# Retention and an ELU feed-forward layer on one core: the blank products at the beginning, and the place of one group of retention products

## The chip, the cores and the metric

The kernel runs on one core of a Trainium2 chip. Its time is the device time of one execution in microseconds (us). The kernel before has a median of 639.2 us over 13 runs, which lie between 636.57 and 641.93. Five engines work side by side: TensorE (PE in the profile; its weight loads are PEld) multiplies matrices, VectorE (DVE) and ScalarE (ACT) work on elements, GpSimd (POOL) does a little of the same, and SyncE (SP) issues the transfers.

## The reference

Two blocks follow one another. Both work in float32.

```python
# retention: q, k, v are (4, 8, 768, 64); one gamma per head
for t in range(S):
    state = gamma * state + einsum('bhd,bhe->bhde', k[:, :, t], v[:, :, t])
    y[:, :, t] = scale * einsum('bhd,bhde->bhe', q[:, :, t], state)
# feed-forward: x is y as (3072, 512)
h = x @ w_in                                        # 512 x 2048
g = np.where(h > 0, h, np.exp(np.minimum(h, 0)) - 1)
out = g @ w_out                                     # 2048 x 512
```

## The kernel before

**Work and stages.** The 3072 tokens are cut into six blocks of 512 (`tb` in the code), and each block into four chunks of 128. For a chunk, retention is computed in sub-chunks of 64 tokens, with products of 64x64: scores (`score_products`, L313), state increments (`state_products`, L344), the part of the output within a sub-chunk (`within`, L400), and the part that comes from the earlier state (`across`, L415). VectorE masks the scores (L324, L334), sums the states (L354, L356) and multiplies the output by powers of gamma into `xb` (L390, L439), which is the input of the feed-forward layer.

The two large products of a block use Strassen's scheme with seven products in place of eight. In the second product of blocks 1 to 5 it is applied twice (`second_twice`): an outer product `j` is made of seven inner ones (`inner`, L955), each of four 128x128 matmuls with weights that were combined before, sent to DRAM and brought back through a ring of eleven buffers (`fetch_small`). VectorE makes the inner inputs (`ts`, L832) and adds the results (L967); ScalarE copies out of PSUM (L963, L988). Between outer products VectorE also combines four inputs (`next_input`, L775).

**What sets the order.** The schedule is manual: each engine executes its instructions in the order in which the Python code emits them, and semaphores between engines follow from the tiles. Generators interleave the stages by hand. The outer products run in the order `ORDER2 = [1, 2, 6, 7, 5, 3, 4]`. `second_twice` yields after each outer product; at such a yield the main loop may place retention work of the next block, a "visit", by `retention_step`. Of an outer product, five inner products come before its yield, and the last two come after the first two of the next. Between two successive yields lie seven inner products.

`retention_step(tb, step)` has five steps: 0 makes the scores, 1 the states. Steps 2, 3 and 4 advance the output: step 2 makes the products L400 and the first half of L415 for the first pair of chunks, with a tiny copy (`seen`, L384) by VectorE that reads both banks; step 3 does the same for the second pair; step 4 makes the second half of L415 for both pairs and the final multiplications (L390). In the loop over blocks 2 to 5, steps 2, 3, 4 for the next block are at the yields numbered 1, 3, 5 of the second product; block 5 has no next block, so this happens three times. Block 1 has a loop of its own with other places, and block 0 another second product.

**The beginning.** No weights are ready at the start: they come as float64 bits in pieces (`load_piece`), which ScalarE and VectorE turn into float32 (L168, L170, L172, L194, L195, L198). TensorE begins with `unread`: products of a tile of zeros (`blank`) whose result nothing reads. Two of 512 columns stand before the scores of chunk 0, one of 256 before its states, and two more of 512 stand further on. Then come the products of chunks 0 and 1, and the plain first product of block 0 (`plain_first`, L503 and L527).

Of the kernel before, what the change touches and what calls it, by code (L numbers as in the profile page):

```python
# [18 lines left out]
def kernel(  # L19
# [32 lines left out]
    nc = tc.nc  # L52
    PSUM = bass.MemoryType.PSUM
    P = nc.NUM_PARTITIONS

    B, H, S, D, DM, DFF = dims
    NTOK = B * S
    C = P
    TB = 512
# [39 lines left out]
    def load(m):  # L99

        if m >= NCHUNK:
            return
        for which in range(2):
            load_one(m, which)
# [106 lines left out]
    blank = hpool.tile([P, TB], FP32, name="blank", tag="h")  # L211
# [69 lines left out]
    def scale_v(m):  # L281
        if m >= NCHUNK:
            return
        i = chunks[m][1]
        qk, kv = raw[m]
        eng = nc.vector if m < 2 else nc.gpsimd
        eng.tensor_tensor(  # L287
            out=kv[:, 1], in0=kv[:, 1], in1=vf[:, i].unsqueeze(2).to_broadcast([C, H, D]), op=ALU.mult
        )
# [28 lines left out]
    def scores(tb, pp):  # L318

        sc = [ps_r.tile([P, 2, HP, D], FP32, name="sc", tag="r") for _ in range(2)]  # L320
        for x in range(2):
            score_products(sc, tb, pp, x)
        for a in range(2):
            nc.vector.tensor_tensor(  # L324
                out=raw[tb * CPB + 2 * pp + a][0][:, 1].rearrange("p h c -> p (h c)").rearrange("p (n t) -> p n t", t=D),
                in0=sc[a].rearrange("p x h t -> p (x h) t"),
                in1=cmask.unsqueeze(1).to_broadcast([P, 2 * HP, D]), op=ALU.mult,
            )
# [29 lines left out]
    def states(tb, pp):  # L358

        kvs = [ps_r.tile([P, 2, HP, D], FP32, name="kv", tag="r") for _ in range(2)]  # L360
        for x in range(2):
            state_products(kvs, tb, pp, x, range(2))
        for x in range(2):
            for sub in range(2):
                state_sum(kvs, tb, pp, x, sub)
# [80 lines left out]
    def outputs_step(tb, step):  # L446

        if step == 0:
            held["y"] = [outputs(tb, pp) for pp in range(2)]
        if step < 2:  # L450
            next(held["y"][step])
            next(held["y"][step])
        else:
            for g in held["y"]:
                next(g, None)
# [3 lines left out]
    def combine_x_parts(tb=None):  # L459
        sub = lambda o, x, y: nc.vector.tensor_tensor(out=o, in0=x, in1=y, op=ALU.subtract)  # L460
        b11, b12, b21, b22 = (x_of(tb)[:, 2 * r : 2 * r + 2, half[t]] for r in range(2) for t in range(2))
        t1, t2, t3, t4_ = xt1 if tb == 1 else xt
        sub(t1, b12, b11)
        yield
        sub(t2, b22, t1)
        yield
        sub(t3, b22, b12)
        yield
        sub(t4_, b21, t2)
# [4 lines left out]
    def flush():  # L474
        while later:
            later.pop(0)()
# [214 lines left out]
    def bank(x):  # L691
        return ps_f.tile([P, 2, TH], FP32, name="p" + x, tag=x, bufs=2 if x == "a" else 1)

    def kept(ps):
        m = mpool.tile([P, 2, TH], FP32, name="m", tag="m")
        nc.scalar.copy(m, ps)  # L696
        return m
# [210 lines left out]
    def first_rest(n, j, ps):  # L908

        w, x = {  # L910
            1: (w_a[n][:, :, 0], xb[:, 0:2, half[0]]), 6: (w_s[n][:, 0], xt[1]), 5: (w_b[n][:, :, 0], xt[0]),
            4: (w_b[n][:, :, 1], xt[3]), 7: (w_s[n][:, 1], xt[2]),
        }[j]
        for fi in range(2):
            for j2 in range(2):
                nc.tensor.matmul(  # L916
                    ps[:, fi, :], lhsT=w[:, fi, j2, :], rhs=x[:, j2, :],
                    start=(j in (1, 7) and fi == 0 and j2 == 0), stop=(j2 == 1), skip_group_check=True,
                )

    def first_end(n, name, ps, x=None):

        g = gq[name][:, 2 * n : 2 * n + 2, :]
        nc.vector.tensor_tensor(out=g, in0=ps, in1=g if x is None else x, op=ALU.add)  # L924
        g = g.rearrange("p a b -> p (a b)")

        def combine():
            mine = lambda x: gq[x][:, 2 * n : 2 * n + 2, :].rearrange("p a b -> p (a b)")
            sub = lambda o, x, y: nc.vector.tensor_tensor(out=o, in0=x, in1=y, op=ALU.subtract)
            sub(mine("T3"), mine("C22"), mine("C12"))  # L930
            sub(mine("T1"), mine("C12"), mine("C11"))

        return lambda: elu(g, g, 3, combine if name == "C22" else None)
# [164 lines left out]

    warm = bank("a").rearrange("p a b -> p (a b)")

    def unread(count, n):
        for _ in range(count):
            nc.tensor.matmul(warm[:, 0:n], lhsT=blank[:, 0:P], rhs=blank[:, 0:n], start=True, stop=True, skip_group_check=True)

    unread(2, TB)
    sc = [ps_r.tile([P, 2, HP, D], FP32, name="sc", tag="r") for _ in range(2)]
    score_products(sc, 0, 0, 0)
    scale_v(0)
# [14 lines left out]
    mask_pair(sc, 1)  # L1123
    scale_v(1)
    unread(1, TB)
    inner = plain_first()
    next(inner)
# [125 lines left out]
    def retention_step(tb, step):  # L1253
        if tb >= NTB:
            return
        if step == 0:
            scores(tb, 0)
            scores(tb, 1)
        elif step == 1:
            states(tb, 0)  # L1260
            states(tb, 1)
        elif step < 5:
            outputs_step(tb, step - 2)
# [51 lines left out]
    for tb in range(2, NTB):  # L1315
        more = tb + 1 < NTB
        qa, qd, u2, end = {}, {}, {}, None

        def rest(n, j):
            if j == 1:  # L1320
                qa[n] = ps_r.tile([P, 2, TH], FP32, name="qa", tag="r") if n == 0 else bank("a")
            if j == 7:
                qd[n] = ps_r.tile([P, 2, TH], FP32, name="qd", tag="r") if n == 3 else bank("bd"[n % 2])
            first_rest(n, j, qa[n] if j in (1, 6, 5) else qd[n])

        def bring(n):
            if more:
                load((tb + 1) * CPB + n)
                scale_v((tb + 1) * CPB + n)

        def pop(count=1):
            for _ in range(count):
                if later:
                    later.pop(0)()

        bring(0)
        rest(0, 1)
        for _ in tail:
            pass
        tail, parts = iter(()), combine_x_parts()  # L1340
        for at, j in enumerate(TWICE):
            cur = first_twice(tb, j)

            next(cur)
            next(tail, None)
            next(parts, None)
            next(cur)
            for _ in tail:
                pass
            next(parts, None)  # L1350
            if at == 1:

                first_end(0, "C11", qa[0])()
                bring(1)
            next(cur)
            tail = cur
        next(tail)
        bring(2)

        sec = second_twice(tb, combine_x_twice if more else lambda: None)  # L1360
        for n in range(NQ):

            rest(n, 6)
            u2[n] = kept(qa[n])
            if n == 0:
                for _ in tail:
                    pass
            if end:
                end()
            pop()  # L1370
            rest(n, 7)
            m7 = kept(qd[n])
            pop(2)
            if n == 2 and more:
                retention_step(tb + 1, 1)
            if n == 3:
                next(sec)
            rest(n, 5)
            end = first_end(n, "C12", qa[n])
            other = first_end(n, "C22", qa[n], m7)  # L1380
            if n < 3:
                end()
                other()
                rest(n + 1, 1)
                first_end(n + 1, "C11", qa[n + 1])()
                rest(n, 4)
                end = first_end(n, "C21", qd[n], u2[n])
                pop()
                if n == 0:
                    bring(3)  # L1390
                elif n == 1 and more:
                    retention_step(tb + 1, 0)
        for _ in range(2):
            next(sec)
        end()
        other()
        rest(3, 4)
        end = first_end(3, "C21", qd[3], u2[3])
        next(sec)
        end()  # L1400
        flush()
        for step, s in enumerate(sec):

            if step in (1, 3, 5):
                retention_step(tb + 1, 2 + step // 2)
            if s == ORDER2[-1]:
                break
        tail = sec
# [51 lines left out]
```

## Time and profile before

| What | Value |
|---|---|
| Median of 13 runs | 639.2 us |
| The profiled execution | 637.46 us |
| Its span, first to last instruction | 635.7 us |
| TensorE products | 626.2 us busy (99%), 6626 records |
| TensorE weight loads | 560.0 us busy (88%) |
| VectorE | 483.0 us busy (76%) |
| ScalarE | 252.8 us busy (40%) |
| GpSimd | 40.3 us busy (6%) |
| Transfers | 136.84 MB, mean 215 GB/s |

The profile shows one execution. A timeline line gives the start, the duration, the engine, the line of the kernel, the operation, the tiles (result <- operands) and shapes, the number of merged records, and in brackets the idle time before it with what ended it. A float32 product makes two records of matmul and two of weight load. Durations of matmuls include their latency, so records overlap: the pace is read from the starts. "issue" is time in which an engine waited for nothing that the profile shows.

### The profile page before, as it was taken

The numbers are of one execution on the slowest core, as the hardware profiler recorded it, in microseconds if no ns is written. First come the engines' busy times: TensorE is split into PE (matmuls) and PEld (weight loads), VectorE is DVE, ScalarE is ACT, GpSimd is POOL, SyncE is SP. The second block draws the span as 40 slices with busy tenths as digits, with TensorE's granted clock in tenths as the row PEclk, the third lists the DMA queues.
The fourth block names the chain that finished last, engine by engine and source line by source line (L and its number), as shares of the span: only waits on it lengthen the run. The fifth ranks groups of instructions, "written<-read, shape, count | busy, mean of one in ns | idle before, by whom it ended". The sixth has DMA issues, their size and how long they took to land.

```text
span 635.7 us, 16093 instructions
## 1 busy us (share of the span) xinstructions
PE 626.2 (99%) x6626; PEld 560.0 (88%) x6626; DVE 483.0 (76%) x870; ACT 252.8 (40%) x472; POOL 40.3 (6%) x42
## 2 busy tenths in 40 slices
PE   8899999999999999999999999999999999999998
PEld 5765568888889999889999989999988999988997
DVE  5769979978989675589676598767489859558975
ACT  6689735114551113554112546111465211356311
POOL 1102000000820000200000100000110000000000
DMA  8789876688486888505889802889820688700794
GB/s 294 305 334 347 279 208 194 203 236 270 139 296 195 277 246 291 218 3 152 276 257 311 282 3 67 254 278 301 293 89 12 205 272 273 233 21 1 222 312 163
DMA packets 79209, 136.84 MB, mean 215 GB/s; under 512 B 6688, under 2 KB 32160, under 8 KB 76960
## 3 DMA queue, kind: packets, MB, share of 16 engines
q1 hardware_dynamic: 79136, 135.82, 65.4%
q8 instruction: 52, 0.85, 0.5%
q14 instruction: 21, 0.17, 0.1%
HBM read 114.56 MB, written 21.23 MB: 214 GB/s over the span
## 4 chain that ended last, share of the span: by engine, by line
PE 95%; DMA 2%; DVE 1%; issue 1%; ACT 1%; SPq 0%; POOL 0%; DVEq 0%
PE pa L955 20%; PE pa L916 10%; PE pd L955 10%; PE pb L955 5%; PE pa L870 5%; PE pb L916 4%; PE pa L527 3%; PE pa L746 3%; PE qa L916 3%; PE x L617 3%; PE pd L870 2%; PE qd L916 2%; PE pa L617 2%; PE pd L916 2%; PE y L400 2%; PE sc L313 2%
## 5 line engine op out<-in xcount | busy, mean ns | idle before, releaser
L963 ACT COPY ms<-pa 128x128 f32<-128x128 f32 x104 | 27.6, 265 | 146.8 <-PE pa L955 145.2
L955 PE MATMUL pa<-ts,wq 128*128 128x128 f32 x560 | 74.1, 275 | 0.3 <-ACT ms L963 0.3
L955 PE MATMUL pd<-ts,wq 128*128 128x128 f32 x552 | 73.2, 275 | 0.0
L955 PEld LDWEIGHTS pa<-ts,wq 128*128 128x128 f32 x560 | 68.5, 192 | 0.8 <-ACT ms L963 0.5
L955 PEld LDWEIGHTS pd<-ts,wq 128*128 128x128 f32 x552 | 67.1, 192 | 0.3 <-DVE res L967 0.2
L955 PE MATMUL pa<-gC,wq 128*128 128x128 f32 x480 | 65.0, 278 | 0.9 <-issue 0.9
L484 ACT ACTIVATE r<-r 128x512 f32<-128x512 f32 x96 | 60.5, 631 | 3.1
L955 PEld LDWEIGHTS pa<-gC,wq 128*128 128x128 f32 x480 | 59.1, 192 | 2.5 <-issue 1.1
L483 ACT ACTIVATE r<-gC 128x512 f32<-128x512 f32 x64 | 39.9, 624 | 32.9 <-DVE gC L924 32.9
L967 DVE TENSOR_TENSOR res<-pd,ms 128x128 f32<-128x128 f32 x68 | 19.5, 287 | 36.8 <-PE pd L955 35.6
L287 POOL TENSOR_TENSOR kvn<-kvn,vf 128x512 f32<-128x512 f32 x22 | 26.1, 1192 | 312.8 <-DMA kvn<-in_qkv_dram 202.4
L487 DVE SCALAR_TENSOR_TENSOR gC<-r,gC 128x512 f32<-128x512 f32 x64 | 44.9, 734 | 0.7 <-ACT r L484 0.7
L832 DVE TENSOR_TENSOR ts<-gC,ts 128x512 f32<-128x512 f32 x60 | 41.3, 688 | 1.0
L832 DVE TENSOR_TENSOR ts<-gC 128x512 f32<-128x512 f32 x60 | 41.0, 684 | 0.0
L955 PE MATMUL pb<-gC,wq 128*128 128x128 f32 x240 | 32.8, 277 | 0.1
L988 ACT COPY res<-pa 128x128 f32<-128x128 f32 x34 | 9.0, 265 | 56.2 <-PE pa L955 54.7
L955 PEld LDWEIGHTS pb<-gC,wq 128*128 128x128 f32 x240 | 29.5, 192 | 0.8 <-DVE gC L487 0.8
L696 ACT COPY m<-pa 128x512 f32<-128x512 f32 x24 | 13.9, 579 | 29.8 <-PE pa L916 13.5
L924 DVE TENSOR_TENSOR gC<-qa,gC 128x512 f32<-128x512 f32 x8 | 5.5, 692 | 25.0 <-PE qa L916 18.3
L916 PE MATMUL pa<-xt,w_b 128*128 128x256 f32 x96 | 23.0, 382 | 0.0
L916 PE MATMUL pa<-xt,w_s 128*128 128x256 f32 x96 | 23.0, 382 | 0.0
L916 PE MATMUL pa<-xb,w_a 128*128 128x256 f32 x96 | 22.7, 379 | 0.0
(253 smaller groups left out, 1251.9 us busy)
## 6 DMA issues: line engine op xcount, KB each, us to landing
wq<-scratch_dram SPq DMA_DIRECT2D x277, 256.0 KB, 4.4
wraw<-in_w_dram SPq DMA_DIRECT2D x15, 1024.0 KB, 7.0
qk<-in_qkv_dram SPq DMA_DIRECT2D x24, 512.0 KB, 6.8
kvn<-in_qkv_dram SPq DMA_DIRECT2D x24, 512.0 KB, 7.4
out_dram<-res SPq DMA_DIRECT2D x14, 256.0 KB, 4.4
scratch_dram<-gT SPq DMA_DIRECT2D x12, 256.0 KB, 4.3
scratch_dram<-m SPq DMA_DIRECT2D x12, 192.0 KB, 6.0
scratch_dram<-so SPq DMA_DIRECT2D x4, 512.0 KB, 4.5
```

Source lines behind the costliest of these rows:

```text
L287: eng.tensor_tensor(out=kv[:, 1], in0=kv[:, 1], in1=vf[:, i].unsqueeze(2).to_broadcast([C, H, D]), op=ALU.mult)
L483: nc.scalar.activation(e, h, AF.Relu, scale=-1.0)
L484: nc.scalar.activation(e, e, AF.Exp, scale=-1.0)
L487: nc.vector.scalar_tensor_tensor(g, e, -1.0, h, ALU.add, ALU.max)
L527: nc.tensor.matmul(hp, lhsT=w[n][:, fi, j // 2, j % 2, :], rhs=xb[:, j, :], start=(j == 0), stop=(j == 3))
L617: nc.tensor.matmul(X[j][:, d, :], lhsT=w[j][:, d * P : d * P + P], rhs=x[j], start=(n == 0 and d == 0), stop=at_end, skip_group_check=True,)
L832: sub = lambda o, x, y: nc.vector.tensor_tensor(out=o, in0=x, in1=y, op=ALU.subtract)
L870: nc.tensor.matmul(ps[:, f, :], lhsT=lhs[f], rhs=xs[j][k], start=(begin and f == 0), stop=True, skip_group_check=True,)
L916: nc.tensor.matmul(ps[:, fi, :], lhsT=w[:, fi, j2, :], rhs=x[:, j2, :], start=(j in (1, 7) and fi == 0 and j2 == 0), stop=(j2 == 1), skip_ ...
L955: nc.tensor.matmul(ps, lhsT=w[:, f, :], rhs=ts[j][k][:, f, :], start=(begin and f == 0), stop=(f == 3), skip_group_check=True,)
L963: nc.scalar.copy(m, ps)
L967: nc.vector.tensor_tensor(out=o, in0=x, in1=y, op=ALU.add)
```

## The change

There are two edits. In the first, `unread` takes the size of the quadratic blank weights as an argument `k`. Of the two 512-column blank products at the very beginning the first stays. In place of the second stand 28 products of 64 rows, 64 columns of weights and 64 moving columns. All 28 read the same corner of `blank` and write the same corner of the same PSUM bank. In the second edit, retention step 3 of the next block moves in the second product of blocks 2, 3 and 4 from the yield numbered 3 to the yield numbered 4; steps 2 and 4 stay at yields 1 and 5.

```diff
-    def unread(count, n):
+    def unread(count, n, k=P):
         for _ in range(count):
-            nc.tensor.matmul(warm[:, 0:n], lhsT=blank[:, 0:P], rhs=blank[:, 0:n], start=True, stop=True, skip_group_check=True)
-
-    unread(2, TB)
+            nc.tensor.matmul(
+                warm[0:k, 0:n], lhsT=blank[0:k, 0:k], rhs=blank[0:k, 0:n], start=True, stop=True, skip_group_check=True
+            )
+
+    unread(1, TB)
+    unread(28, D, D)
     sc = [ps_r.tile([P, 2, HP, D], FP32, name="sc", tag="r") for _ in range(2)]
     score_products(sc, 0, 0, 0)
     scale_v(0)
...
         for step, s in enumerate(sec):
 
-            if step in (1, 3, 5):
-                retention_step(tb + 1, 2 + step // 2)
+            if step in (1, 4, 5):
+                retention_step(tb + 1, {1: 2, 4: 3, 5: 4}[step])
             if s == ORDER2[-1]:
                 break
         tail = sec
```

In the order of TensorE's instructions, the 48 products of step 3 (32 of L400 and 16 of L415; 32 and 12 for block 4, whose first sub-chunk of a sequence has no earlier state) now come 28 matmuls of L955 later. On VectorE, the two copies L384 come behind the four combinations L832 of the next outer product. The orders of ScalarE, GpSimd and SyncE stay as they are.

## The prediction

> **What bounds the kernel now.** I read the page's busy row first, then the start and the second matrix product in the timeline, then the chain that ended last, and then the waits.
>
> ```profile
> PE 626.2 (99%) x6626; PEld 560.0 (88%) x6626; DVE 483.0 (76%) x870; ACT 252.8 (40%) x472; POOL 40.3 (6%) x42
> ...
> q8 instruction: 52, 0.85, 0.5%
> ```
>
> TensorE is busy for 626.2 of 635.7 us, so a change gains or loses only where TensorE idles, or by giving it more to do. Second line: 52 packets of instructions came in, 0.85 MB, about 16 KB each. TensorE runs 13,506 instructions (6,626 products, as many weight loads, 254 others)[...].
>
> The start, in the timeline (start, duration, engine, line, tiles, shape):
>
> ```profile
> 1.45 3.78 PE L1103 MATMUL pa<-blank 128*128 128x512 f32 x4 [1.45 <-DVE blank L212]
> 5.16 1.13 PE L313 MATMUL sc<-qk 64*64 64x64 f32 x32
> 6.22 0.87 PE L1103 MATMUL pa<-blank 128*128 128x256 f32 x2
> 7.03 0.69 PE L344 MATMUL kv<-kvn 64*64 64x64 f32 x32
> ...
> 8.30 0.45 PE L415 MATMUL pd<-qk,kvn 64*64 64x64 f32 x8
> ...
> 11.49 1.12 PE L503 MATMUL pa<-xb,w_a 128*128 128x128 f32 x8
> ```
>
> The two large blank products are four records (float32 takes two passes). Passes two to four start 0.853 us apart; the last leaves the array at 5.02, and the scores (L313) follow at 5.16. At 7.03 the state products (L344) wait for VectorE's scaling of v (L287, 6.22 to 6.91), and that for its load. All before about 6.5 us runs at half speed: 32 small products take 1.13 us at 5.16 but 0.69 at 7.03, though the granted clock reads 1.00 in every row.
>
> The only long idle times of TensorE, in the chain in order of time:
>
> ```profile
> 25.40 1.07 PE y L400 x58
> 26.47 1.72 issue
> 28.20 0.28 PE y L400 x3
> ```
>
> ```profile
> 503.84 0.98 PE pa L955 x7
> 504.81 0.94 issue
> ```
>
> "issue" means that no semaphore explains the wait. By start stamps the losses are 1.9 us (26.25 to 28.19) and 1.1 us (504.54 to 505.75). In the packet records of the instruction queue, a packet begins at 25.67 and lasts 1.07, another at 503.32 and lasts 0.92; both idle times end 1.5 us after their packet. Counting TensorE's instructions, these two stops and a 0.2 us one ending at 14.22 fall on counts equal modulo 256. They are waits for code[...].
>
> The second matrix product, around the visit that moves:
>
> ```profile
> 315.65 1.16 PE L400 MATMUL y<-qk,kvn 64*64 64x64 f32 x64
> 316.63 0.65 PE L415 MATMUL y<-qk,kvn 64*64 64x64 f32 x32
> 317.21 1.16 PE L955 MATMUL pa<-gC,wq 128*128 128x128 f32 x8
> ...
> 320.89 1.06 PE L955 MATMUL pa<-ts,wq 128*128 128x128 f32 x8
> ...
> 329.91 1.15 PE L415 MATMUL y<-qk,kvn 64*64 64x64 f32 x56
> ```
>
> ```profile
> 316.02 0.68 DVE L832 TENSOR_TENSOR ts<-gC,ts 128x512 f32<-128x512 f32 x1
> ...
> 317.31 0.24 DVE L384 COPY seen<-y 128x8 f32<-128x8 f32 x2 [0.41 <-PE y L415]
> ...
> 325.82 0.69 DVE L832 TENSOR_TENSOR ts<-gC,ts 128x512 f32<-128x512 f32 x1
> ```
>
> TensorE takes a product every 0.89 us without a hole, on both sides of the visit.
>
> **The change, part by part.**
>
> *Blank products.* Removed: two passes of 0.853, 1.71 us. Added: 28 float32 products, 56 passes, all on one 64x64 quarter. Such a stream is not in the trace. Floor: the four-quarter stream of L313, (1.13-0.31)/31 = 0.026 us a pass (0.31 is one record's latency), 1.5 us, no delay. Ceiling: weight load and product in turn, twice 0.107, 12 us at half speed. L313 gives each quarter 8 of its 32 passes, with starts within a quarter 0.107 us apart; at full speed (L344) 0.058. The two-quarter stream at 8.30 takes longer per pass than the four-quarter one, so the quarter is the limit, and loads are hidden in all of them. I take 0.107. Starting at 3.46 (free at 3.32 plus the 0.14 seen at 5.02 to 5.16), with the clock rising at 6.5 as now, 28 passes run slow and 28 at 0.058: end about 8.1, scores 8.2, **3.0 us late**.
>
> What covers it: the scores run at full speed and the state products waited until 7.03 for v anyway. Scores end 8.7, the blank 256-column product (0.43 warm) 9.1, so L344 is at 9.1, 2.1 late, and VectorE's first "seen" copy at 10.7 instead of 8.80. Behind that copy VectorE is nearly continuous to 11.33 (L439 twice, L356, L195, L198), and L503 at 11.49 needs the last of these. So **+1.9 us** reaches the first matrix product. The 0.44 wait for the second q, k load at 9.9 does not cover it, as VectorE decides.
>
> *Code blocks.* 27 more products, four instructions each: 108. Every later block boundary falls 108 instructions earlier in the work. [...] The rows show 3.0 us lost, so I count it:
> - At 26 us: the boundary moves 54 passes forward, to the start of the y burst, needed at 25.4+1.9 = 27.3. [...] I take 1.0, so 0.9 is given back.
> - [...] It is now needed after 3.4: +0.4.
> - At 504.5: the boundary before moves from about 499 to 493, with 9.7 us to the next instead of 5.2. Stall gone: -1.1.
> - Near 200: a boundary moves from after the state burst to before it[...]. Between 0 and +1.4; I take +0.4[...].
> - All other gaps stay above 5 us[...]: +0.1.
>
> *The visit, three times.* 48 products (1.55 us) go behind the seven products of the next visited step (6.25 us). Same instructions, same two changes of array shape, no DMA of its own; the weight loads that SP issues behind those products go out 1.55 us sooner, against landings of 4.4 us with 11 buffers: hidden. Those seven products now start at 315.65. The first that reads VectorE's new sums (pa<-ts) moves from 320.9 to 319.3; its last sum (L832) ends at 316.7: 2.6 us to spare. The copies of L384 go behind the L832 ending at 326.5, less up to 1.5; they are read from 329.9: over 3 us to spare. The L967 queued behind them feeds a bank reused two products later. The final multiplications (L390) stay in place. **0**; without that cover a late L384 would cost its lateness, at most about 1 us per block. Bounds -0.3 to +0.5 in all.
>
> *Sum* in the profiled execution's time: +1.9 -0.9 +0.4 -1.1 +0.4 +0.1 = **+0.8**, so 635.7 becomes 636.5 of span and 637.46 becomes 638.3. The median of the runs lies 1.7 above that execution; the difference carries over: **639.2 + 0.8 = 640.0 us**. A measurement tells about 0.2% (1.3 us) from no change, so this counts as no change.
>
> **The rivals.**
> 1. *The clock stays low* (slower). If products on one quarter do not count as enough activity, all 56 passes take 0.107 and end at 9.45, and scores, states and y run at half speed behind them: "seen" at 13.9, +5.1. Then loads are ahead and the 26 us stall goes: 5.1-1.9-1.1+0.5 = +2.6, **641.8**. For it: the low clock itself. Against: [...] no row here shows a quarter alone. It decides once the rise slips past 9.4; each microsecond before that costs 0.46.
> 2. *Code waits come back* (slower). The y burst stalls 2.0, the next block 0.8, the burst at 200 1.4: 1.9+0.1+0.8-1.1+1.4 = +3.1, **642.3**. [...]
> 3. *Code waits vanish* (faster). The new boundaries meet no burst: 1.9-1.9-0.2-1.1 = -1.3[...]: **637.6**. If the small products stream at the floor instead, there is no delay and the same side is reached: the edit is then a mere move of boundaries.
>
> **How the numbers follow.** Forecast (640.0) 0.36, its own range 638.6 to 640.9; rival 1 0.20, rival 2 0.18, rival 3 0.26. Faster is rival 3, slower is 1 and 2: 0.26, 0.36, 0.38. One in ten lies below 636.8, within rival 3, and one in ten above 642.7, within 2.
>
> **What would show it.** Right: L313 near 8.2 and L503 (128x128) near 13.4; an issue wait of about 1 us moved to the front of the y burst near 27; none at 504; visits without holes. Wrong: L313 near 5.2 (floor), or 64x64 records still long after 9 us (rival 1); issue waits over 1 us near 200 or 330 (rival 2); any VectorE wait ahead of L415 or pa<-ts near 320. Failing first would be the single-quarter pace or the arrival at 27, which I inferred rather than saw.

## The result and the profile after

The changed kernel takes **643.7 us** (median of 11 runs, 642.24 to 644.53) against 639.82 for the kernel before (48 runs, 636.25 to 642.28). The ratio is **1.0066, with a 95% interval of 1.0048 to 1.0085**: slower by 4 us, outside the predicted range. The profiled execution took 644.97 us with a span of 643.1, which is 7.4 us more span than before.

The 7.4 and the 4 differ because the mean granted clock of TensorE differs between executions. The profiled execution after had one stretch of 3.413 us (207.91 to 211.32 in the clock's records) at half the clock, and a mean of 0.997; half of that stretch, 1.7 us, is the estimate of its cost. The kernel before had a mean of 0.997 or lower in 64 of the 114 runs measured beside the experiments, the changed one in 2 of 12. The profiled execution of before had 1.000. Runs of before with that clock lie near 637.1 (median of 14, measured together with e5), those of the changed kernel near 643.8 (10 of 12). So at an equal clock the change costs about 6.7 us, and the profiled execution after, about 5.8 without its stretch.

The busy row and the instruction queue of the page after:

```profile
PE 633.8 (99%) x6680; PEld 567.5 (88%) x6680; DVE 483.3 (75%) x870; ACT 252.7 (39%) x472; POOL 39.7 (6%) x42
...
q8 instruction: 53, 0.87, 0.5%
```

TensorE is busy 7.6 us longer, so the loss lies in busy time rather than in waits, which nearly balance. The 56 small passes at full speed would be 56 x 0.058 = 3.2 us, less the 1.7 of the large ones, or 1.5; e5 below shows 3.0 us of the rest to be the low clock at the start, and 1.6 more are the half clock near 208 us. There is one more packet of instructions (53 for 52).

The start, in the timeline of after:

```profile
1.45 8.13 PE L1103 MATMUL pa<-blank 128*128 128x512 f32 x57 [1.45 <-DVE blank L212]
9.28 0.38 PE L313 MATMUL sc<-qk 64*64 64x64 f32 x3
9.38 0.31 PE L1103 MATMUL pa<-blank 64*64 64x64 f32 x1
9.44 1.10 PE L313 MATMUL sc<-qk 64*64 64x64 f32 x29
10.47 1.22 PE L1103 MATMUL pa<-blank 128*128 128x256 f32 x2
11.62 1.13 PE L344 MATMUL kv<-kvn 64*64 64x64 f32 x32
...
13.38 0.41 PE L415 MATMUL pd<-qk,kvn 64*64 64x64 f32 x8
...
16.51 1.13 PE L503 MATMUL pa<-xb,w_a 128*128 128x128 f32 x8 [0.49 <-DVE w_a L198]
```

VectorE's first `seen` copy, before and after:

```profile
8.80 0.16 DVE L432 COPY seen<-pd 128x4 f32<-128x4 f32 x1 [0.55 <-PE pd L415]
```

```profile
13.83 0.16 DVE L432 COPY seen<-pd 128x4 f32<-128x4 f32 x1 [0.55 <-PE pd L415]
```

The state products (L344) took 0.69 before and take 1.13 now, and the blank product of 256 columns 1.22 where it took 0.87: half speed. The clock's records say full speed from 13.35 us. L415 at 13.38 is the first group that runs about as before (0.41, before 0.45). VectorE's `seen` copy starts at 13.83 instead of 8.80, and the first matrix product at 16.51 instead of 11.49: 5.0 us late.

The chain around the y burst, and the visit in the second product of block 2:

```profile
28.71 1.92 PE pd L503 x8
30.64 1.09 PE y L400 x64
```

```profile
329.54 1.06 PE L955 MATMUL pa<-ts,wq 128*128 128x128 f32 x8
330.53 1.16 PE L400 MATMUL y<-qk,kvn 64*64 64x64 f32 x64
...
332.09 1.16 PE L955 MATMUL pa<-gC,wq 128*128 128x128 f32 x8
```

The wait of 1.7 us inside the y burst is gone altogether. The moved visit has no hole on either side. What is new comes near 206 us:

```profile
203.90 2.07 PE L344 MATMUL kv<-kvn 64*64 64x64 f32 x110
207.53 0.27 PE L344 MATMUL kv<-kvn 64*64 64x64 f32 x2 [1.55 <-issue]
207.73 1.94 PE L955 MATMUL pa<-gC,wq 128*128 128x128 f32 x8
...
211.16 1.13 PE L955 MATMUL pa<-gC,wq 128*128 128x128 f32 x8
```

A burst of 56 small products, 112 passes, stops after 110 passes for a wait that no semaphore explains, and behind it TensorE is granted half its clock for 3.413 us (207.91 to 211.32 in the clock's records): eight passes of L955 take 1.94, and 1.13 once the clock is back.

With start times of the same products subtracted (after minus before; places are times of the kernel before), the difference grows like this: scores +4.12, first matrix product +5.02, at 19.4 us +5.29, behind the y burst +3.2, at 190 us +5.2 (0.58 at 54, 0.33 at 67, 0.39 at 79, 0.60 at 181, all at small waits or their edges), behind the wait at 206 and the half clock +8.6, behind 504.5 us +7.4, and so to the end.

### The profile page after: what moved, and what is told of

It reads as the page before. It is cut to its first block, busy times and chain, and to the rows that moved or that the text cites. A ratio compares the mean times of both kernels' runs of the same rounds, so it can differ in the third digit from the quotient of the medians.

```text
span 643.1 us, 16201 instructions
## 1 busy us (share of the span) xinstructions
PE 633.8 (99%) x6680; PEld 567.5 (88%) x6680; DVE 483.3 (75%) x870; ACT 252.7 (39%) x472; POOL 39.7 (6%) x42
## 4 chain that ended last, share of the span: by engine, by line
PE 90%; DVE 3%; ACT 2%; issue 2%; POOL 1%; DMA 1%; POOLq 0%; SPq 0%; DVEq 0%
PE pa L955 20%; PE pa L916 10%; PE pd L955 9%; PE pb L955 5%; PE pa L870 5%; PE pb L916 4%; PE qa L916 3%; PE x L617 3%; PE pa L527 2%; PE pd L870 2%; PE qd L916 2%; PE pd L916 2%; PE pa L617 2%; PE kv L344 2%; PE y L400 2%; PE sc L313 2%
## 5 line engine op out<-in xcount | busy, mean ns | idle before, releaser
L955 PE MATMUL pa<-ts,wq 128*128 128x128 f32 x560 | 74.1, 275 | 0.3 <-ACT ms L963 0.3
L955 PE MATMUL pd<-ts,wq 128*128 128x128 f32 x552 | 73.1, 275 | 0.0
L955 PEld LDWEIGHTS pa<-ts,wq 128*128 128x128 f32 x560 | 68.5, 192 | 0.8 <-ACT ms L963 0.5
L955 PEld LDWEIGHTS pd<-ts,wq 128*128 128x128 f32 x552 | 67.1, 192 | 0.3 <-DVE res L967 0.2
L955 PE MATMUL pa<-gC,wq 128*128 128x128 f32 x480 | 65.6, 280 | 0.4 <-DMA wq<-scratch_dram 0.4
L955 PEld LDWEIGHTS pa<-gC,wq 128*128 128x128 f32 x480 | 59.8, 194 | 2.0 <-issue 0.7
L287 POOL TENSOR_TENSOR kvn<-kvn,vf 128x512 f32<-128x512 f32 x22 | 25.5, 1164 | 321.6 <-DMA kvn<-in_qkv_dram 295.7
L832 DVE TENSOR_TENSOR ts<-gC,ts 128x512 f32<-128x512 f32 x60 | 41.3, 688 | 1.0
L832 DVE TENSOR_TENSOR ts<-gC 128x512 f32<-128x512 f32 x60 | 41.0, 684 | 0.0
L955 PE MATMUL pb<-gC,wq 128*128 128x128 f32 x240 | 33.7, 282 | 0.1
L955 PEld LDWEIGHTS pb<-gC,wq 128*128 128x128 f32 x240 | 30.4, 197 | 0.8 <-DVE gC L487 0.8
L696 ACT COPY m<-pa 128x512 f32<-128x512 f32 x24 | 13.9, 579 | 30.0 <-PE pa L916 13.7
```

Source lines behind the costliest of these rows:

```text
L287: eng.tensor_tensor(out=kv[:, 1], in0=kv[:, 1], in1=vf[:, i].unsqueeze(2).to_broadcast([C, H, D]), op=ALU.mult)
L955: nc.tensor.matmul(ps, lhsT=w[:, f, :], rhs=ts[j][k][:, f, :], start=(begin and f == 0), stop=(f == 3), skip_group_check=True,)
```

## The experiments

The question that the profile leaves is how the start (+5.0) divides into the time of the small products and the low clock, what keeps the clock low, and whether the waits further on come from the number of instructions. "Start" below is the start of the scores, "seen" VectorE's first copy; differences are taken against the profiled execution of before.

### e2 and e1: one edit alone

```diff
-            if step in (1, 3, 5):
-                retention_step(tb + 1, 2 + step // 2)
+            if step in (1, 4, 5):
+                retention_step(tb + 1, {1: 2, 4: 3, 5: 4}[step])
```

> The visit alone, the start as before. If the clock at the start is the cause: within 0.3% of the kernel before (-1 to +1 us), no holes in TensorE around the visits. If the moved visit is the cause: +2 us or more, with VectorE waits ahead of the products L955 or L415 near 320, 420 and 520 us.

The visit alone (e2): 638.36 against 639.13, ratio 1.0003 (0.9982 to 1.0024), end of the profile -0.06 us. **The visit costs nothing.** The end alone would not show it, for two waits cancel there: a wait of 1.36 us at 13.8, in the products of block 0, where the kernel before had 0.22 (+1.1), and the wait at 504.5 us, which was absent (-1.2). But the difference stays at +1.15 from 215 to 500 us, over two of the three moved visits, and at -0.05 over the third. The wait at 504.5 was also absent in e8, e10 and e11, where the code is not shifted by 108 instructions: it is not a steady part of the kernel before, and its loss is no gain of the shift.

```diff
-    unread(2, TB)
+    unread(1, TB)
+    unread(28, D, D)      # unread with k, as in the change
```

> The blank products alone, the visit where it was. If the low clock after the blank products is the cause: scores at 9.3 us, full speed only after about 13 us, and nearly all of the loss of the whole change, +3 to +4.5 us. If the moved visit is the cause: less than +1. [...]

The blank products alone (e1): 645.83 against 639.13, ratio 1.0096 (1.0061 to 1.0131). Start at 9.28 as in the changed kernel, full clock at 14.10, seen at 14.09, the wait near 206 again and a half clock of 3.413 us behind it. The whole loss belongs to this edit, and it is larger than the expected +3 to +4.5.

### e3: the same 28 products over four quarters

```diff
-    unread(28, D, D)
+    for n in range(28):
+        r, c = rows(n % 2), rows(n // 2 % 2)      # the two halves
+        nc.tensor.matmul((warm, warm2)[n % 2][c, 0:D], lhsT=blank[r, 0:D], rhs=blank[r, 0:D], ...)
```

> Both edits, with the same 28 small products dealt round over the four quarters of the array (7 each), in two banks. Same number of instructions, so the same code blocks. If the pace of one quarter and the clock behind it are the cause: the blank products end near 5.0, the scores start near 5.2, full speed at about 6.5 as before, and the whole loss at the start goes: within -2 to +0.5 us of the kernel before (the waits for code move, the one near 504 us should be gone). If the 108 more instructions are the cause, the loss stays at +3 or more.

The instructions are as many as in the change; only the places in the array differ. 640.05 against 639.13, ratio 1.0014 (0.9996 to 1.0033). Start 5.0, seen 8.73, first matrix product within 0.01 us of before. The timeline and, further on, the chain of e3:

```profile
5.01 0.78 PE L313 MATMUL sc<-qk 64*64 64x64 f32 x32
```

```profile
200.59 2.00 PE kv L344 x110
202.59 1.27 issue
```

The scores run at full speed (0.78 for 32 passes), so the whole start goes with the single quarter. What remains is the shift of 108 instructions by itself: -0.2 up to 19.4 us, -1.7 over the y burst, +0.6 in the product behind it, +2.4 between 65 and 80 us, +0.7 at 181, +1.5 near 200, +0.2 near 232, -1.2 at 504: +2.35 at the end, where at most +0.5 was expected. The stop near 200 comes **after the same 110 passes** as in the changed kernel.

That number is the test for the waits. In all five kernels that have 108 instructions more (the change, e1, e3, e5, e6), the burst breaks after pass 110, for 1.55, 1.82, 1.27, 1.82 and 0.72 us, however late they are there (1.8 to 10.6 us). In e2, e8 and before it runs through; e2's timeline:

```profile
199.87 2.08 PE L344 MATMUL kv<-kvn 64*64 64x64 f32 x112
```

So in these eight kernels the place goes with the count of instructions and not with the time. The traces of before and after show more. They hold three idle times of TensorE of over 0.7 us that no semaphore explains: 26.47 to 28.20 and 504.81 to 505.75 before, 205.98 to 207.53 after. Ahead of their ends the traces hold 962, 11,202 and 4033 instructions of TensorE, counts that lie multiples of 256 apart to within one. They end 1.4 to 1.5 us after the end of a packet of the instruction queue (26.74, 504.25 and 206.17). That they are waits for code is the author's reading of these times. What sets the length of one (0.72 to 1.82 us at the same place in the five kernels) was not shown.

### e7: half the shift

```diff
-    for n in range(28):      # of e3
+    for n in range(14):
```

> As the four-quarter kernel, but with 14 small products in place of 28: code blocks move by 52 instructions in place of 108, no delay at the start. If the waits follow the block boundaries: a wait of 1 to 2.5 us inside the first y burst (near 25 to 28) that the 28 did not have, and the wait near 203 in the state burst falls from 1.5 to under 0.8. If the waits are chance: no such pattern. Time within -1 to +1.5 us of the kernel before.

640.1 against 638.3, ratio 1.0025 (1.0006 to 1.0044); the profiled execution ended 0.67 us earlier than before. The wait in the y burst did move forward, as expected, to the middle of L400 (it ends at 26.99), but cost 0.35 us and not 1 to 2.5: a miss in size. The burst near 200 runs through, and a stop that costs 1.2 us appears in the y burst that follows, ending at 209.1.

### e8: the same columns on one quarter in few instructions

```diff
-    unread(28, D, D)
+    unread(3, TB, D)
+    unread(1, TH, D)
```

> As the changed kernel, but in place of the 28 products three of 512 and one of 256 moving columns on the same quarter of the array: the same 1792 columns, so the same 6.0 us at half speed, with 16 instructions for 112. If the quarter decides the clock: scores at 9.3, full speed at 13 us, seen at 13.8, +5 us at the first matrix product, and since the code blocks stay nearly where they were, the wait in the y burst (now near 31) stays in place of being given back: at 60 us about +4.5 to +5.3 against +3.7 in the changed kernel, and no wait of 1.5 us in the state burst near 205. If many small instructions decide the clock: full speed at 5.5 to 7.

The 1792 moving columns are those of the 28 products, in four long ones, so that only 12 instructions are added in place of 108. 644.97 against 638.3, ratio 1.0089 (1.0054 to 1.0124). The timeline of e8:

```profile
9.48 1.06 PE L313 MATMUL sc<-qk 64*64 64x64 f32 x26
...
34.07 0.39 PE L400 MATMUL y<-qk,kvn 64*64 64x64 f32 x10 [1.36 <-issue]
...
36.17 3.33 PE L503 MATMUL hp<-xb,w_a 128*128 128x256 f32 x8
```

The clock rises even later than the expected 13 us (18.41; seen 14.08, first matrix product +6.16): four long products on the quarter brought it no sooner than 28 small ones. The wait in the y burst is back (1.36) and the one near 200 is gone. Behind the wait, the clock is granted at half from 35.48 to 38.89 (L503: 3.33 for eight passes instead of 1.99): end +8.2.

### e5, e9 and e11: which half of the array

```diff
-    unread(28, D, D)
+    for _ in range(28):                               # e5: 128 rows x 64 columns
+        nc.tensor.matmul(warm[0:D, 0:D], lhsT=blank[:, 0:D], rhs=blank[:, 0:D], ...)
```

```diff
-    unread(28, D, D)
+    for n in (TB, TB, TB, TH):                        # e9: 64 rows x 128 columns
+        nc.tensor.matmul(warm[:, 0:n], lhsT=blank[0:D, 0:P], rhs=blank[0:D, 0:n], ...)
```

```diff
-    unread(1, TB)
-    unread(28, D, D)
+    for n in (TB, TB, TB, TB, TH):                    # e11: 128 rows x 64 columns, from the first
+        nc.tensor.matmul(warm[0:D, 0:n], lhsT=blank[:, 0:D], rhs=blank[:, 0:n], ...)
```

> As the changed kernel, but each of the 28 small products uses 128 rows and 64 columns of weights: half the array for a quarter, same number of instructions, same moving columns. If the clock counts how much of the array works: full speed may come at about 5.5 to 7 us, the small products end near 8, scores near 8.1, first seen copy near 10.7, and about 2 us less than the changed kernel at the first matrix product. If half is still too little, or if many small instructions are what keeps the clock low: full speed at 13 us again, scores at 9.3, seen at 13.8.

> Both edits, but in place of the 28 small products three of 512 and one of 256 moving columns, the same 1792 columns, with 64 rows x 128 columns of blank weights: two quarters of the array side by side, where 128 rows x 64 columns had two above each other. The number of instructions is that of the kernel before but for twelve. If the clock goes by the share of the array that works, whichever way it lies: full clock near 5.4, scores near 7.6, first 'seen' near 10.8, L503 near 13.4 (+1.9 against before), the wait in the y burst stays, end +1.5 to +3. If only the rows count (one row half is too little): clock low to 13 or later, scores near 9.3, first 'seen' near 14, L503 near 17, end +6 to +8 as with the long products on one quarter.

> Both edits, but the blank products at the beginning, the first large one too, are all 128 rows x 64 columns of weights: four of 512 and one of 256 moving columns, so that no product on the whole array stands before the scores. With 64 rows x 128 columns the clock stayed low; with 128 rows x 64 columns it rose at 5.48[...]. If the rows that are fed decide: full clock between 4.9 and 8.3, scores between 7.0 and 8.9, first 'seen' between 10.2 and 12, L503 between 12.8 and 14.7, end +1.5 to +4. If the share of the array decides and half is too little: clock low until after the scores, scores at 9.3 to 9.8, full clock at 12.5 to 16, first 'seen' near 14, L503 near 16.7, end +5 to +8.

Timelines of e5, e9 and e11, in this order (a float32 product makes two passes):

```profile
3.45 4.38 PE L1109 MATMUL pa<-blank 128*64 128x64 f32 x56
7.77 0.69 PE L313 MATMUL sc<-qk 64*64 64x64 f32 x32
```

```profile
3.46 6.34 PE L1109 MATMUL pa<-blank 64*128 64x512 f32 x8
9.72 1.13 PE L313 MATMUL sc<-qk 64*64 64x64 f32 x32
```

```profile
1.45 5.57 PE L1108 MATMUL pa<-blank 128*64 128x512 f32 x10 [1.45 <-DVE blank L212]
6.95 0.69 PE L313 MATMUL sc<-qk 64*64 64x64 f32 x32
```

| | rows x columns | full clock at | start | L503 against before | ratio (interval) |
|---|---|---|---|---|---|
| change | 64 x 64 | 13.35 | 9.28 | +5.02 | 1.0066 (1.0048 to 1.0085) |
| e5 | 128 x 64 | 5.48 | 7.77 | +1.98 | 1.0062 (1.0037 to 1.0087) |
| e9 | 64 x 128 | 12.70 | 9.72 | +5.23 | 1.0065 (1.0038 to 1.0092) |
| e11 | 128 x 64 | 4.48 | 6.95 | +1.19 | 1.0026 (1.0004 to 1.0048) |

e5 and e9 use the same share of the array, yet e5 has the full clock at 5.48 and e9 at 12.70; e11 has it at 4.48 without any product on the whole array (the clock, the scores, `seen` and L503 all came slightly ahead of the ranges expected for it). **In these runs products on 128 rows and 64 columns had the full clock 7 to 8 us sooner than products on 64 rows and 128 columns.** e5 is also the changed kernel with the same 28 products and the same instructions, but with the clock at 5.48: it shows that of the 5.0 us at the start, 2.0 are the time of the small products and 3.0 the low clock. Its end in the profile is +5.17, as it met the waits of the shift in nearly full size (+1.42 behind the y burst, +2.04 near 200). The ratios of e5 and the change can't be told apart, for the runs of before measured with e5 have a median of 638.3 (mean clock 0.997 or lower in 11 of 26); at a granted clock of 1.000, e5 costs about 4.2 us (641.3, median of 5, against 637.1) and the change about 6.7.

### e6 and e4: the whole array

```diff
-    unread(28, D, D)
+    unread(28, D)        # e6: 128 x 128 weights, 64 moving columns
```

> As the changed kernel, but the 28 small products use the whole array (128 rows, 128 columns of weights, 64 moving columns). If the share of the array decides: full speed at about 5.5 to 7 us and the products end at 8 to 9 (a weight load of 128 columns may set their pace). If many small instructions keep the clock low: full speed only [...]at 12 us or later.

```diff
-    unread(1, TB)
-    unread(28, D, D)
+    unread(6, TB)        # e4: six large products, whole array
```

> Both edits, but six blank products of 512 columns over the whole array in place of one large and 28 small: they end at about 9.2, as the 28 do, if the clock rises at 6.5. If the low clock is a cause of its own: scores start near 9.2 as in the changed kernel, but run at full speed, the first seen copy comes at about 11.8 instead of 13.8, and the time lies about 2 us below the changed kernel (+1 to +2.5 against before). If only the later start counts: the same loss as the changed kernel, +4.

e6: 649.1 against 638.3, ratio 1.0184 (1.0147 to 1.0221). Timeline:

```profile
1.45 13.91 PE L1103 MATMUL pa<-blank 128*128 128x512 f32 x58 [1.45 <-DVE blank L212]
15.29 1.13 PE L313 MATMUL sc<-qk 64*64 64x64 f32 x32
```

A pass takes (15.29 - 3.46)/56 = 0.211 us, twice as long as with 64 columns of weights (0.107), though it moves the same 64 columns. A blank weight load of 128 columns takes 0.34 us where it stands alone (2.47 in the trace of before), one of 64 columns 0.22 on average in the trace of after; that the loads set the pace of e6 is an estimate from these times. The clock stayed low until 19.45, though all 128 rows and all columns are used. At half clock 512 columns pass in 0.853 us, so 64 in 0.107, about half of the 0.211: by this estimate columns move for only half of the time. That this kept the clock low was not shown.

e4: 642.75 against 639.13, ratio 1.0057 (1.0028 to 1.0086). The clock rose at 5.36 and the scores began at 8.72, 3.6 us late, of which 2.9 reached the first matrix product. This is what a late start at full clock costs here (32 scores take 0.69). The end was +5.18 in the profile rather than +2.9, and also above the expected +1 to +2.5. About 1.3 us of that come near 20 us, where TensorE waits 0.71 and 0.52 us for VectorE's conversion (L198). VectorE of e4:

```profile
19.60 1.41 DVE L198 CUSTOM_DVE_ANT_0 w_a<-wraw,w_a 128x1024 uint16<-128x1024 uint16 x1
```

L198 takes 0.69 in the kernel before and 1.41 here, where GpSimd's multiplication (L287, 19.32 to 20.46) had begun first, and a second one 1.31 behind the next L287. In the kernel before another instruction of VectorE, L194, met the same L287 at 19.27 and took 1.27 instead of 0.42, off the critical path. Most of the rest (about 1.0 us) comes at 424 and 504 us of the kernel before.

### e10: nothing in place of the small products

```diff
-    unread(28, D, D)
```

> Both edits, but the 28 small products left out and nothing in their place: one large product, then the scores. If what the change costs at the beginning is the time of the small products and the low clock that they leave, and not the missing second large product: scores near 4.7 (their load decides), full clock between 5.4 and 6.5 from the scores on four quarters, L503 within 0.4 of 11.5, the wait in the y burst within 0.3 of before (four instructions fewer), end -0.7 to +0.5. If the second large product is what lifts the clock: full clock at 8 or later, first 'seen' at 9.5 to 10.5, L503 at 12.2 to 13.2, end +0.7 to +2.

```profile
4.79 1.13 PE L313 MATMUL sc<-qk 64*64 64x64 f32 x32 [1.26 <-DMA qk<-in_qkv_dram]
...
13.02 1.27 PE L503 MATMUL pa<-xb,w_a 128*128 128x128 f32 x8
```

In this timeline the scores begin as soon as their load is there, 0.4 us before the kernel before, and still the first matrix product is 1.5 us late: the clock came only at 13.45. The second expectation was right: without the second large product in the 1.3 us in front of the scores the full clock came at 13.45, where in the kernel before the state products at 7.03 already took 0.69. The profiled execution ended +1.55, but the runs lie between 637.4 and 651.3 with a median of 646.6; the ratio of the eight quickest of 14 is 1.0051 (1.0011 to 1.0090) and leaves the others out. Their mean granted clock falls on the whole as the time rises, from 1.000 to 0.989; what lies behind that in them no trace shows.

None of these kernels is faster than the kernel before.

## Why the prediction was wrong

The forecast was no change; the result is a slower kernel, by the mechanism of rival 1 and with a part of rival 2 on top. What failed is the rise of the clock at 6.5 us, on which the sum for the start stands.

- **The pace of the single quarter: right.** Taken 0.107 us a pass at half speed; measured (9.38 - 3.46)/55 = 0.108.
- **"With the clock rising at 6.5 as now": the step that failed.** It rose at 13.35. All 56 passes ran slowly (0.108 us) and so did the scores and states (1.13 us for 32 states). Scores +4.12 instead of +3.0, `seen` at 13.83, first matrix product +5.02 instead of +1.9. Rival 1 had said 13.9 and +5.1. And e5, the same products where the clock does rise, came to +1.98: the forecast's +1.9 was a correct sum on a wrong premise.
- **What stood against rival 1.** The forecast took the early rise for granted with a quarter at work as well; no row of before showed a quarter alone. In the change, e8 and e9 the array was busy without a hole from 3.46 to beyond 9.4 us, and the clock stayed low until 13.35, 18.41 and 12.70. The row at hand, slow 64x64 products at the beginning (1.13 for 32 at 5.16), could not decide it, for products on the whole array were as slow there (two passes of 512 columns take 2.08 us at 1.45 in e9, 1.12 at 15.11).
- **At 26 us: right in place, too small.** When a packet of instructions is there in time was the author's estimate. Taken -0.9; measured -2.0 in all five kernels with the shift, e3 included, whose start is not late. So the stall of 1.0 that the sum kept at the front of the burst never came, with or without the late start. The block behind it: +0.4 taken; 0 in the change, e1 and e6, which are five us late or more, but +0.6 in e3 and +1.42 in e5.
- **Near 200 us: the right place, too small.** Taken +0.4, an estimate from a range of 0 to 1.4. Measured +1.77 in the change and 0.94 to 2.04 in the other four with that shift: above the upper end in four of the five. Rival 2 had 1.4.
- **"All other gaps": too small.** +0.1 taken, +1.9 measured, at 54, 67, 79 and 181 us. Not all of it is idle time that no semaphore explains: the piece at 54 ends with VectorE's `gC` (a wait of 0.31) and the one at 181 with the transfer of `wq` (0.37), though the latter came in all five kernels with the shift and in no other. e3, where the start is unchanged, had +3.7 there and at the block behind the y burst. Of the 53 packets of instructions in the trace of the change only one goes with an idle time of over 0.7 us that no semaphore explains, the one in the burst near 206; the four pieces here are 0.33 to 0.60 each.
- **The half clock behind a wait: not in the sum at all.** +1.6 in the profiled execution. It is also why "the difference carries over" failed: by the granted clocks, the 1.7 us between the median of before and its profiled execution go with a lower clock (runs of before at 0.997 lie near 639.7, at 1.000 near 637.2), and the changed kernel had a mean of 0.997 less often (2 of 12 against 64 of 114).
- **At 504: -1.1 taken, -1.2 measured, for the wrong reason.** e2 loses this wait without any shift: luck.
- **The visit: 0, right.** In e2 no difference arises over any of the three moved visits.
- **Small slips.** Rival 3's own terms give 637.9 and not 637.6; and the "32 small products" of a row are 16 products of two passes each.

The sum in the profile: +5.0 +0.3 (to 19.4 us) -2.0 +1.9 +1.8 +1.6 -1.2 = +7.4. Rival 1's own sum ended at +2.6 because its terms for the code were as small as those of the forecast.

## What to carry to other kernels

Products that are there to lift TensorE's clock are worth trying first on all 128 rows, with many moving columns each. Here 128 rows x 64 columns had the full clock at 4.48 (512 moving columns) and 5.48 us (64), half the rows at 12.70 or later, in few long products as in many small ones; but 28 products of 64 moving columns on the whole array, with a pass every 0.211 us, had it only at 19.45. (All blank products here multiply zeros; other values were not tried.) If instructions are added ahead of a manual schedule with bursts of 64x64 products, look at each burst: with 108 more, the state burst near 200 got a wait of 0.7 to 1.8 us and the y burst near 26 lost one of 1.7. Add the shift alone (as e3 does) to see its price apart from the price of the work. And when a sum is made against one profiled execution, look at that execution's granted clock and at those of the runs before carrying it over to the median.

## What the hardware showed that was not expected

- Products on 64 rows without pause left the clock at half for long: full speed came at 13.35 and 14.10 (64 x 64; the change and e1), 18.41 (64 x 64 in long products) and 12.70 us (64 x 128). With 128 x 64 it came at 5.48 and 4.48 us. With small products on the whole array, a pass every 0.211 us, it came at 19.45.
- A wait inside a burst of 64x64 products could be followed by half clock: 1.55 us (the change) and 1.82 (e1) in the burst near 206, 1.36 (e8) and 2.12 (e11) in the y burst. The stretch lasted 3.413 us in the change (207.91 to 211.32) and 3.41 in e8 (35.48 to 38.89). It isn't certain to follow: e3, e5 and e9 had waits of 1.27, 1.82 and 1.30 us without it. What decides stays open.
- VectorE's conversion (L198) took 1.41 instead of 0.69 us where a GpSimd multiplication had begun first; where L198 began first (18.66 against 19.06 in the kernel before), it kept its 0.69.
- The granted clock of the changed kernel's profile does not show the slow start: every row of the windows up to 13 us reads 1.00, while 32 passes of L344 at 11.62 take 1.13 us for 0.69, and the first record of the clock is at 13.35. Durations of a known shape show the low clock.
